# Scatters of token rows that no longer wait for one another's landing, and half of the kv copies on VectorE

## The chip, the cores and the metric

The kernel runs on one core of a Trainium2 chip. The metric is the device time of one execution in microseconds. Three runs of the kernel before took 650.41, 650.43 and 651.4 us; their median is 650.43 us. A profile of one execution shows when each engine worked: TensorE (PE, and PEld for its weight loads), VectorE (DVE), ScalarE (ACT), GpSimd (POOL) and SyncE (SP), which issues the plain loads.

## The reference

A linear attention without a softmax feeds a mixture of experts. Batch is 8, heads 8, sequence 576, head width 64; there are 8 experts of 512 to 1024 to 512.

```python
kv = np.einsum('bhsd,bhse->bhde', k, v)
out = np.einsum('bhsd,bhde->bhse', q, kv)
rms = np.sqrt(np.mean(out * out, axis=-1, keepdims=True) + 1e-06)
x = (out / rms * g_norm)                 # to (B, S, 512)
logits = np.einsum('bsd,de->bse', x, w_gate)
local_gate = 1.0 / (1.0 + np.exp(-(x @ w_local)))
# for each batch, for s in order:
fresh_e = int(np.argmax(logits[b, s]))
e = fresh_e if s == 0 or local_gate[b, s] < 0.5 else prev_e
h = np.maximum(x[b, s] @ w1[e], 0.0)
out[b, s] = softmax(logits[b, s])[e] * (h @ w2[e])
```

So each of the 4608 tokens goes through one expert, and which one is known only when its logits are.

## The kernel before

The first stage works on two batches and two heads at a time: 16 steps (`NST`), four steps (`NP`) to a group of two batches, four groups (`NGRP`). For each step s, `kv(s)` multiplies k and v on TensorE, and ACT copies the result from PSUM (`kvp`, line 390: 128 partitions, of which the lower 64 belong to the first batch of the pair and the upper 64 to the second). `kvb_of(s, t)` at line 404 lays it out in a matrix `kvb` that the product with q reads. It makes four copies per step, all on POOL: t says which half of the partitions is written, b which half is read. In the order of the program: lower half to lower half, upper to lower, lower to upper, upper to upper. ACT adds the logits' columns to the same matrix (line 431), and only then goes on to its other copies. `q_kv(s)` multiplies (lines 462, 467 and 473), and ACT writes the rows to `raw`, nine chunks (`C`) of 128 tokens for a group. POOL and ACT square them (line 511 is POOL's share), VectorE sums them (line 516).

When a group has its four steps, `rows_out` and `route` compute on VectorE which expert each token takes and at which place of a sorted list in DRAM (`xs_sorted`) its row goes (line 716). `scatter` (line 586) then writes one chunk of 128 rows with an indirect DMA from POOL. There are 36 scatters, nine to a group. Each writes the same DRAM tensor as the one before, so each waits until that one has landed.

The second stage takes rows back from `xs_sorted` with gathers. The first blocks of 128 rows of expert 0 are processed with fixed places: `ready(b)` gathers block b (line 733) and needs the groups 0 to b scattered; `scale0` scales the rows on VectorE (line 778) and `turn` transposes them on TensorE (line 790). The four blocks are called a, b, c and d here. Then come the experts 1 to 7 in the order of their numbers of rows, with `gather4` (line 745).

The order of the program is written out by hand, as strings of letters: one letter is one piece of work, and `work_of` looks up what it means. Each engine runs its own instructions in that order. The letters that matter: `0` and `1` are `kvb_of` for the next step, `n` is POOL's square of the step before, `o` is `scatter(3)`, `G` in step 14 is the scatters that are still due (they also wait for the last load of q). `LATE` replaces the string of the last steps; in steps 8 to 11 it appends a letter, in steps 8 to 10 a second `o`. In block a the string `PASS` puts seven scatters of group 2 at `a8`, in block b nine of group 3 at `b7`; `r` at `a6`, `b6` and `c3` is the gather for the next block.

As group 0 is placed at the end of step 7, its nine scatters stand six in step 8 and three in step 9. Group 1 is placed at the end of step 11: three scatters in step 12, six at `G`. Group 2: two in step 15, seven at `a8`. Group 3: nine at `b7`.

Of the kernel before, what the change touches and what calls it, by code (L numbers as in the profile page):

```python
# [22 lines left out]
def kernel(  # L23
# [14 lines left out]
    B, H, S, D = q.shape  # L38
# [7 lines left out]
    C = S // D  # L46
    W = C // 2
    NP = H // 2
    HW = D + NG
    PW = 2 * HW  # L50
    KB = PW - NG
    XO = NG
    NGRP = B // 2
    NCH = NGRP * C
    NST = NGRP * NP
# [9 lines left out]
    CLOSE = {g: g + 1 for g in range(NGRP - 1)}  # L65
    IDC = 1

    QUARTERS = range(NST - NP - 1, NST)


# [65 lines left out]
    KVB, LGC = "PP", "A"  # L136
# [150 lines left out]
    def load_q(s, b):  # L287
        if s < NST:
            qts[s, b] = load(q, lq, "qt", s, b)
# [45 lines left out]
    for x in range(2):  # L335
        rows = slice(x * D, (x + 1) * D)
# [9 lines left out]
    for b in range(2):  # L346
        rows = slice(b * D, (b + 1) * D)
# [24 lines left out]
    kvps, kqs, qTs, qls = {}, {}, {}, {}  # L372

    def half(b):
        return slice(b * D, (b + 1) * D)
# [17 lines left out]
    def blocks(s, t, o, dims):  # L393

        v_ = kvbs[s % 3][half(t), o + t * HW:]
        return bass.AP(v_.tensor, v_.offset, [v_.ap[0], *dims])

    def slot(x, b):
        return (2 * b + x) * PW

    def kvb_of(s, t):

        for b in range(2):
            copy[KVB[t]](blocks(s, t, slot(0, b) + XO, [(PW - XO, 2), (1, D)]), kvps[s][half(b)])  # L404
        done.add((s, t))

    copy = {"A": nc.scalar.copy, "D": nc.vector.tensor_copy, "P": nc.gpsimd.tensor_copy}
# [36 lines left out]
    def q_kv(s):  # L444
# [9 lines left out]
        def part(w0):  # L454
            po = ps_o.tile([P, 2, 512], F32, name="po")
            for w in range(w0, w0 + 2):
                for x in range(2):
                    for r in range(2 if s in QUARTERS else 0):
                        for b in range(2):
# [3 lines left out]
                                             kvb[half(r), o:o + HW], start=True, stop=True)  # L463
                    for b in range(0 if s in QUARTERS else 2):
                        out = po[half(b), w - w0, 0:2 * PW].rearrange("p (r e) -> p r e", r=2)
# [3 lines left out]
            if w0:  # L469
                for x in range(2):  # L470
                    for b in range(2):
# [6 lines left out]
                           po[:, :, 0:2 * PW].rearrange(  # L478
                               "p r (w e) -> p w r e" if s in QUARTERS else "p w (r e) -> p w r e",
                               e=PW))  # L480
# [4 lines left out]
        return part(0), part(2)  # L485

    bg = {}
    to_place, placed, unread = [], [], []
    done = set()

    def adv(g, n=1):

        for _ in range(n):
            while next(bg[g][0], "end") == "end":
                bg[g].pop(0)
                if not bg[g]:
                    return
# [80 lines left out]
    def scatter(n=C, after=None):  # L578

        for _ in range(min(n, len(to_place))):  # L580
            g, c, raw = to_place.pop(0)
            if not c:
                nc.gpsimd.tensor_copy(
                    raw.rearrange("p c (a w) -> p c a w", w=PW)[:, :, :, IDC],
                    tid[:, g].unsqueeze(2).to_broadcast([P, C, NP]))
            i = nc.gpsimd.indirect_dma_start(  # L586
                out=xs, out_offset=bass.IndirectOffsetOnAxis(
                    ap=place[:, g * C + c:g * C + c + 1], axis=0),
                in_=raw[:, c].bitcast(I32), in_offset=None, bounds_check=E * SPAN - 1, oob_is_err=False)
            while blank:  # L590
                tc.add_manual_dep(i.ins, blank.pop().ins.name, mybir.DependencyInfo(
                    mybir.DependencyClass.Sync, mybir.DependencyReason.DATA))
            if after:
                tc.add_manual_dep(i.ins, after.ins.name, mybir.DependencyInfo(
                    mybir.DependencyClass.Sync, mybir.DependencyReason.DATA))
                after = None
            placed.append((g, c))
            unread.append(i)

    def sum_last(dst, src):  # L600
        with nc.allow_low_precision("whole numbers below 2 ** 17"):
# [129 lines left out]
    def gather(xr, idx, groups=NGRP):  # L731
        assert len(placed) >= groups * C
        i = nc.gpsimd.indirect_dma_start(
            out=xr.bitcast(I32), out_offset=None, in_=xs,
            in_offset=bass.IndirectOffsetOnAxis(ap=idx, axis=0),
            bounds_check=E * SPAN - 1, oob_is_err=False)
        while unread:
            tc.add_manual_dep(i.ins, unread.pop().ins.name, mybir.DependencyInfo(
                mybir.DependencyClass.Sync, mybir.DependencyReason.DATA))
        return xr  # L740

    def gather4(xr, r, k, u):

        assert not unread
        i = nc.gpsimd.indirect_dma_start(  # L745
            out=xr[:, u * PW:(u + 1) * PW].bitcast(I32), out_offset=None,
            in_=xs.rearrange("t (q w) -> (t q) w", w=PW),
            in_offset=bass.IndirectOffsetOnAxis(ap=gid4[:, r - 2, u * KBM + k:u * KBM + k + 1], axis=0),
            bounds_check=E * SPAN * NP - 1, oob_is_err=False)
        if behind:  # L750
            tc.add_manual_dep(i.ins, behind.pop().ins.name, mybir.DependencyInfo(
                mybir.DependencyClass.NoSync, mybir.DependencyReason.DATA))
# [52 lines left out]
    def group(g):  # L805
# [7 lines left out]

    STEP = "Q01aKkLlnopTVsqUemwvcRYb"
    EARLY = {-1: "01TLlUeKkV", 0: "Q0aRcT1LlYUeoKkV"}
    LATE = {NST - 8: STEP + "o", NST - 7: STEP + "o", NST - 6: STEP + "o",
            NST - 5: STEP + "2", NST - 4: STEP + "34",
            NST - 3: "Q01aKkLlnTVsqUmcRYX", NST - 2: "Q01GLlTUaspcRXY",
            NST - 1: "QapwcRvosXY"}
    SLOTS = {}  # L820
# [12 lines left out]
    def work_of(i, what):  # L833


        new, nxt, now = i + 2 < NST, 0 <= i + 1 < NST, i >= 0
        if what in "pmqb":
            for g in SLOTS.get((i, what), ()):
                adv(g)
        elif what == "s" and i > 0:  # L840
            for x in range(2):
                sums(i - 1, x)
            if i % NP == 0:
                group(i // NP - 1)
        elif what == "Q" and now:
            step["a"], step["c"] = q_kv(i)
            next(step["a"])
        elif what == "R" and now:
            next(step["c"])
        elif what in "ac" and now:  # L850
            next(step[what])
            done.add((i, what))
        elif what == "K" and new:
            step["k"] = kv(i + 2)
            next(step["k"])
            for b in range(2):
                load_kv(i + 2 + LB, b)
        elif what == "k" and new:
            next(step["k"])
        elif what == "L" and nxt:  # L860
            step["l"] = logits_of(i + 1)
            next(step["l"])
        elif what == "l" and nxt:
            next(step["l"])
            done.add((i + 1, "l"))
        elif what in "01" and nxt:
            kvb_of(i + 1, int(what))
        elif what == "T" and nxt:
            for b in range(2):
                turn_q(i + 1, b)  # L870
        elif what == "U" and nxt:
            turn_last(i + 1)
        elif what == "e" and nxt:
            assert i + 1 in qls and i + 1 in qTs
            for b in range(2):
                load_q(i + 1 + LQ, b)
            if i + 1 + LQ == NST - 1:
                for x in range(len(LOADED), NW1 + NW2):
                    wload(0, x)
        elif what == "V" and new:  # L880
            turn_kv(i + 2)
        elif what == "w" and i in SPLIT:
            step["v"] = wsplit(0, SPLIT[i], True)
        elif what == "v" and i in SPLIT:
            step.pop("v")()
        elif what == "n" and i > 0:
            squares(i - 1, 0)
        elif what in "XY" and now:
            squares(i, "XY".index(what), True)
        elif what == "o":  # L890
            if i in LOADED:
                wload(0, LOADED[i])
            elif i < NST - 1:
                scatter(3)
            else:
                scatter(2)
        elif what == "G":
            right.close()
            wpool("c")
            wpool("d")  # L900
            scatter(after=latest["qt"])
        elif what == "2":
            ready(0, sm)
        elif what == "3":
            scale0(0)
        elif what == "4":
            turn(*e0[0], 0, ps_q, "pq")
# [16 lines left out]
    for i in range(-2, NST):  # L924
        if i == NST - 1:
            paced.clear()
        for what in {**EARLY, **LATE}.get(i, STEP):
            work_of(i, what)
# [384 lines left out]
    for bl in la:  # L1313
# [4 lines left out]
    i = first_block(KST - 1, {  # L1318
        2: [split[0]], 4: [split[1]], 7: [split[2]], 8: [split[3]],
        **{11 + x: [bl.scale] for x, bl in enumerate(la[:2])}, 13: [turns[0], la[2].scale],  # L1320
        14: [turns[1]], 15: [turns[2]]}, (hh, hl))
# [111 lines left out]
```

## Time and profile before

| | us |
|---|---|
| median of 3 runs (650.41 to 651.4) | 650.43 |
| the profiled execution | 648.12 |
| its span | 646.4 |
| PE busy | 554.5 (86%) |
| DVE busy | 301.3 (47%) |
| POOL busy | 264.5 (41%) |
| ACT busy | 241.6 (37%) |

The span is the time from the first to the last instruction of the profile; the profiled execution's own time is 1.7 us longer. Busy time is summed over instructions. The page cuts the span into 40 slices of 16 us: in the fifth to fifteenth slice (65 to 242 us) PE's busy share is between 1 and 7 tenths, and from the sixteenth on it is 9 tenths or more. The DMA engines are busy for 9 tenths in the first five slices.

### The profile page before, as it was taken

What the parts mean: (1) busy time and instruction counts of PE and PEld (TensorE: products, weight loads), DVE (VectorE), ACT (ScalarE), POOL (GpSimd) and SP (SyncE); (2) the same over time, 40 slices, a digit from 0 to 9 for tenths busy, and PEclk for the clock granted to TensorE, in tenths of its full rate; (3) what the DMA queues carried; (4) which work ended last, traced back from release to release, by engine and by line L of the source; (5) the groups of instructions that cost most, each with busy time, mean ns of one, the idle gap of its engine ahead of it and who ended that gap; (6) DMA issues with size and microseconds to landing.
All of it is one profiled execution on the core that took longest, in us unless ns stands there. A gap on an engine that the chain in (4) does not pass through costs nothing.

```text
span 646.4 us, 12084 instructions
## 1 busy us (share of the span) xinstructions
PE 554.5 (86%) x4720; PEld 484.1 (75%) x4720; DVE 301.3 (47%) x705; ACT 241.6 (37%) x442; POOL 264.5 (41%) x336
## 2 busy tenths in 40 slices
PE   8999515675664449999999999999999999999996
PEld 5778414564443337989898988989998898998995
DVE  1147313557242017626464637465663763756520
ACT  2678312656111125333333343433443334344321
POOL 5333233343232335627252725734544563561011
PEclk9999857989785869999999999999999999999999
DMA  9999925612243227354233423523443353352000
GB/s 325 348 345 351 348 96 184 205 68 117 93 143 148 108 70 267 105 169 129 90 111 117 129 99 121 161 74 134 133 122 122 128 161 104 130 175 77 6 33 27
DMA packets 37648, 94.96 MB, mean 147 GB/s; under 512 B 5817, under 2 KB 5817, under 8 KB 37582
## 3 DMA queue, kind: packets, MB, share of 16 engines
q1 hardware_dynamic: 26848, 61.88, 28.1%
q0 software_dynamic: 10688, 32.20, 15.0%
q8 instruction: 39, 0.64, 0.4%
q14 instruction: 27, 0.22, 0.1%
q10 hardware_dynamic: 46, 0.02, 0.0%
HBM read 73.85 MB, written 20.88 MB: 147 GB/s over the span
## 4 chain that ended last, share of the span: by engine, by line
PE 67%; issue 16%; DMA 7%; POOL 5%; ACT 1%; DVE 1%; POOLq 1%; another core or an unknown queue 0%; DVEq 0%; ACTq 0%
PE ph L947 10%; PE ph L948 10%; PE ph L942 10%; PE py L948 9%; PE py L942 9%; PE py L947 9%; DMA xs_sorted<-raw,place 5%; POOL xs_sorted L586 4%; PE po L467 3%; PE po L386 2%; PE py L995 1%; DMA xr<-xs_sorted,gi 1%; DMA out_dram<-ot,si 1%; PE pq L441 1%; PE rbank L325 1%
## 5 line engine op out<-in xcount | busy, mean ns | idle before, releaser
L745 POOL DMA_INDIRECT xr<-xs_sorted,gid x120 | 132.8, 1107 | 38.4 <-issue 35.7
L981 POOL DMA_INDIRECT out_dram<-ot,si x38 | 40.2, 1058 | 182.1 <-ACT ot L980 113.1
L1016 DVE SCALAR_TENSOR_TENSOR hl<-ph,hh 128x384 fp32r<-128x384 f32 (+3 forms) x88 | 49.5, 562 | 101.7 <-ACT hh L1015 101.7
L1015 ACT ACTIVATE hh<-ph 128x384 fp32r<-128x384 f32 (+3 forms) x88 | 44.5, 505 | 115.2 <-PE ph L948 115.2
L586 POOL DMA_INDIRECT xs_sorted<-raw,place x36 | 36.0, 999 | 87.3 <-DMA xs_sorted<-raw,place 80.4
L516 DVE TENSOR_REDUCE ms<-sq 128x9 f32<-128x576 f32 x32 | 22.6, 748 | 70.1 <-POOL sq L511 69.9
L778 DVE TENSOR_TENSOR xr<-xr 128x512 f32<-128x512 f32 x40 | 27.5, 687 | 40.6 <-DMA xr<-xs_sorted,gi 40.1
L790 PE MATMUL pt<-ident,xr 128*128 128x128 f32 x40 | 8.1, 337 | 44.2 <-DVE pe L917 38.3
L980 ACT ACTIVATE ot<-py,pe 128x512 f32<-128x512 f32 (+1 forms) x37 | 25.3, 684 | 53.5 <-issue 27.0
L790 PEld LDWEIGHTS pt<-ident,xr 128*128 128x128 f32 x40 | 5.7, 171 | 46.8 <-issue 39.0
L412 PE MATMUL pt<-ident,kvp 128*128 128x128 f32 x16 | 5.0, 313 | 29.3 <-ACT kvb L431 28.1
L404 POOL COPY kvb<-kvp 64x128 f32<-64x128 f32 x64 | 18.8, 294 | 25.5 <-ACT kvp L390 12.5
L467 PE MATMUL po<-kvb,qT 128*64 128x146 f32 x352 | 28.7, 309 | 0.0
L477 ACT COPY raw<-po 128x584 f32<-128x584 f32 x32 | 20.4, 639 | 15.2 <-PE po L473 12.7
L386 PEld LDWEIGHTS po<-vt,kt 64*64 64x64 f32 x1152 | 21.9, 142 | 5.6 <-issue 3.1
L386 PE MATMUL po<-vt,kt 64*64 64x64 f32 x1152 | 24.8, 230 | 1.4 <-issue 1.0
L412 PEld LDWEIGHTS pt<-ident,kvp 128*128 128x128 f32 x16 | 2.3, 145 | 30.4 <-ACT kvb L431 28.8
L771 ACT CAST yh<-xT 128x512 fp32r<-128x512 f32 x17 | 10.5, 620 | 38.8 <-DVE xT L767 38.8
L467 PEld LDWEIGHTS po<-kvb,qT 128*64 128x64 f32 x352 | 22.5, 145 | 3.2 <-issue 2.0
L511 POOL TENSOR_TENSOR sq<-raw 128x576 f32<-128x576 f32 x13 | 15.0, 1154 | 23.8 <-ACT raw L482 12.1
L948 PE MATMUL py<-w_0h,hl 128*128 128x512 f32 (+1 forms) x54 | 21.8, 404 | 3.1 <-DVE hl L1080 3.0
L794 ACT CAST th<-pt 128x512 fp32r<-128x512 f32 x4 | 2.3, 586 | 54.0 <-PE pt L790 54.0
(404 smaller groups left out, 1765.7 us busy)
## 6 DMA issues: line engine op xcount, KB each, us to landing
wst<-in_moe_w_dram SPq DMA_DIRECT2D x64, 512.0 KB
kt<-in_k_dram SPq DMA_DIRECT2D x32, 288.0 KB
vt<-in_v_dram SPq DMA_DIRECT2D x32, 288.0 KB
qt<-in_q_dram SPq DMA_DIRECT2D x32, 288.0 KB
xr<-xs_sorted,gid POOLq DMA_INDIRECT x120, 4.2
out_dram<-ot,si POOLq DMA_INDIRECT x40, 3.9
xs_sorted<-raw,place POOLq DMA_INDIRECT x36, 2.8
xr<-xs_sorted,gi POOLq DMA_INDIRECT x10, 6.6
```

The lines of the kernel that those rows point to most:

```text
L386: nc.tensor.matmul(pk[half(b), x, 0:D], ks[b][half(x), cd], vs[b][half(x), cd], start=(c == 0), stop=(c == C - 1))
L467: nc.tensor.matmul(out[:, :, x * HW:(x + 1) * HW], qT[:, b, w, half(x)], kvb[:, o:o + PW], start=True, stop=True)
L586: i = nc.gpsimd.indirect_dma_start(out=xs, out_offset=bass.IndirectOffsetOnAxis(ap=place[:, g * C + c:g * C + c + 1], axis=0), in_=raw[:, ...
L745: i = nc.gpsimd.indirect_dma_start(out=xr[:, u * PW:(u + 1) * PW].bitcast(I32), out_offset=None, in_=xs.rearrange("t (q w) -> (t q) w", w=PW),
L778: (engine or nc.vector).tensor_mul(xv, xv, r.unsqueeze(3).to_broadcast([P, NP, 2, D]))
L942: mm = nc.tensor.matmul(ps, ah, bh, start=(first and i == 0), stop=False)
L947: nc.tensor.matmul(ps, ah, bl, start=False, stop=False)
L948: nc.tensor.matmul(ps, al, bh, start=False, stop=(last and i == n - 1))
L980: nc.scalar.activation(ot[0:m], po[0:m], AF.Copy, scale=pe[0:m])
L981: return nc.gpsimd.indirect_dma_start(out=outf, out_offset=bass.IndirectOffsetOnAxis(ap=idx[0:m], axis=0), in_=ot[0:m], in_offset=None, bo ...
L1015: nc.scalar.activation(hh, ps, AF.Relu)
L1016: nc.vector.scalar_tensor_tensor(hl, ps[:, :, 0:nl], 0.0, hh[:, :, 0:nl].bitcast(F32), op0=ALU.max, op1=ALU.subtract)
```

## The change

Four things change. In `scatter`, a scatter is declared independent of all earlier scatters and gathers ("other rows"); in `gather`, a gather is declared independent of the scatters of later groups, and keeps its dependence on those of the groups that it reads. In the steps whose `kvb_of` has s from 8 to 13 (`CROSS`, `NP` is 4), the two copies with b = 1 go to VectorE. A letter `o` is now four scatters and does nothing from step 12 on, except two in step 15. The second `o` of steps 8 to 10 is gone. So group 0's nine scatters stand 4, 4 and 1 in steps 8, 9 and 10, and group 1's nine all at `G` in step 14.

```diff
+    CROSS = range(2 * NP, 3 * NP + 2)
...
-            copy[KVB[t]](blocks(s, t, slot(0, b) + XO, [(PW - XO, 2), (1, D)]), kvps[s][half(b)])
+            copy["D" if b and s in CROSS else KVB[t]](blocks(s, t, slot(0, b) + XO, [(PW - XO, 2), (1, D)]), kvps[s][half(b)])
...
-            placed.append((g, c))
-            unread.append(i)
+            for other in moves:
+                tc.declare_no_dep(i.ins, other.ins, reason="other rows")
+            moves.append(i)
+            placed.append(i)
...
-        while unread:
-            tc.add_manual_dep(i.ins, unread.pop().ins.name, mybir.DependencyInfo(
-                mybir.DependencyClass.Sync, mybir.DependencyReason.DATA))
+        for other in placed[groups * C:]:
+            tc.declare_no_dep(i.ins, other.ins, reason="rows of later groups")
+        moves.append(i)
...
-    LATE = {NST - 8: STEP + "o", NST - 7: STEP + "o", NST - 6: STEP + "o",
-            NST - 5: STEP + "2", NST - 4: STEP + "34",
+    LATE = {NST - 5: STEP + "2", NST - 4: STEP + "34",
...
-            elif i < NST - 1:
-                scatter(3)
-            else:
+            elif i < 3 * NP:
+                scatter(4)
+            elif i == NST - 1:
                 scatter(2)
```

## Rows read from the trace of the kernel before

**Rows 1.** The page, chain that ended last: shares of the span by engine.

```profile
PE 67%; issue 16%; DMA 7%; POOL 5%; ACT 1%; DVE 1%; POOLq 1%; another core or an unknown queue 0%; DVEq 0%; ACTq 0%
```

**Rows 2.** PE's waits, 60 to 240 us: total us, times, longest us.

```profile
PE pt L790 <- DVE pe L917: 38.3, 3, 17.9
PE pt L412 <- ACT kvb L431: 28.1, 3, 19.9
PE pt L790 <- issue: 5.5, 1, 5.5
...
PE pl L420 <- ACT kvb L431: 0.7, 1, 0.7
```

**Rows 3.** Timeline of POOL, steps 8 and 9: start, us, engine, line, idle before.

```profile
66.09 1.10 POOL L586 DMA_INDIRECT xs_sorted<-raw,place  x1 [0.29 <-POOL raw L583]
71.43 0.99 POOL L586 DMA_INDIRECT xs_sorted<-raw,place  x1 [4.24 <-DMA xs_sorted<-raw,place]
77.61 0.97 POOL L586 DMA_INDIRECT xs_sorted<-raw,place  x1 [5.20 <-DMA xs_sorted<-raw,place]
...
90.42 0.32 POOL L404 COPY kvb<-kvp 64x128 f32<-64x128 f32 x1
92.39 0.99 POOL L404 COPY kvb<-kvp 64x128 f32<-64x128 f32 x3 [1.66 <-DMA xs_sorted<-raw,place]
```

**Rows 4.** The scatters' line, L586: what POOL waited for, and landing.

```profile
  DMA xs_sorted<-raw,place: 80.4, 30
...
DMA to landing us min/median/max: 2.8/2.8/8.1
```

**Rows 5.** Timeline of ACT in step 9.

```profile
72.49 0.27 ACT L390 COPY kvp<-po 128x128 f32<-128x128 f32 x1 [0.32 <-PE po L386]
92.72 0.18 ACT L431 COPY kvb<-pm 64x36 f32<-64x36 f32 x1 [19.96 <-POOL kvb L404]
```

**Rows 6.** Timeline of POOL, small copies at L583, step 14, and a gather.

```profile
65.55 0.25 POOL L583 COPY raw<-tid 128x36 f32<-128x36 f32 x1
...
139.97 1.03 POOL L586 DMA_INDIRECT xs_sorted<-raw,place  x1 [0.28 <-POOL kvb L404]
...
158.16 1.18 POOL L583 COPY raw<-tid 128x36 f32<-128x36 f32 x1
...
242.75 1.01 POOL L733 DMA_INDIRECT xr<-xs_sorted,gi  x1 [0.31 <-issue]
```

**Rows 7.** Timeline of PE: two steps, a restart, block a's start, three transposes.

```profile
57.26 1.22 PE L467 MATMUL po<-kvb,qT 128*64 128x146 f32 x16
...
63.38 1.22 PE L467 MATMUL po<-kvb,qT 128*64 128x146 f32 x16
...
94.83 2.21 PE L467 MATMUL po<-kvb,qT 128*64 128x146 f32 x16
...
146.03 0.51 PE L942 MATMUL ph<-w_0h,th 128*128 128x512 f32 x1
...
171.88 1.12 PE L790 MATMUL pt<-ident,xr 128*128 128x128 f32 x4 [6.26 <-DVE pe L917]
...
202.48 1.09 PE L790 MATMUL pt<-ident,xr 128*128 128x128 f32 x4 [14.22 <-DVE pe L917]
...
235.12 1.09 PE L790 MATMUL pt<-ident,xr 128*128 128x128 f32 x4 [17.86 <-DVE pe L917]
```

**Rows 8.** The chain in order of time: a gather, issue to landing.

```profile
230.81 3.48 DMA xr<-xs_sorted,gi
```

**Rows 9.** Timeline of DVE: a copy, a two-input instruction, group 3's places.

```profile
100.11 0.15 DVE L568 COPY raw<-r 128x72 f32<-128x72 f32 x1
...
158.01 1.23 DVE L227 TENSOR_TENSOR w_1l<-wst,w_1h 128x1024 fp32r<-128x1024 f32 x1
...
180.58 0.23 DVE L716 TENSOR_REDUCE place<-rk 128x9 int32<-128x72 f32 x1
```

**Rows 10.** A 20 us window: busy us of PE, PEld, DVE, ACT, POOL; granted clock; DMA.

```profile
80.00:100.00 20.00, 6.21 (x113) 4.76 (x115) 3.85 (x10) 5.22 (x12) 6.41 (x10) 0.55 0.36 124
```

More of the change, by code (lines that the diff above doesn't have):

```diff
@@ L487 @@
     bg = {}
-    to_place, placed, unread = [], [], []
+    to_place, placed, moves = [], [], []
     done = set()
@@ L736, in gather @@
             bounds_check=E * SPAN - 1, oob_is_err=False)
-        while unread:
-            tc.add_manual_dep(i.ins, unread.pop().ins.name, mybir.DependencyInfo(
-                mybir.DependencyClass.Sync, mybir.DependencyReason.DATA))
+        for other in placed[groups * C:]:
+            tc.declare_no_dep(i.ins, other.ins, reason="rows of later groups")
+        moves.append(i)
         return xr
     def gather4(xr, r, k, u):
-        assert not unread
         i = nc.gpsimd.indirect_dma_start(
```

## The prediction

> **What bounds the kernel now.** I read the chain of waits first, then TensorE's waits in the stretch that the chain points at, then POOL's timeline there. Over the whole span the chain is two thirds PE [rows 1], so most of the kernel is already bound by TensorE; the rest is "issue", DMA and POOL, and all of that lies between 66 and 235 us. TensorE's waits there show two kinds of stall [rows 2]. In the attention steps it stands 28.1 + 0.7 us behind ACT's L431; in the expert-0 blocks it stands 38.3 us, in three waits, behind VectorE's scaling of gathered rows. Both lead to one place. POOL's timeline shows each scatter followed by an idle time that ends with the landing of the scatter before it [rows 3]: 30 waits, 80.4 us, with a landing of 2.8 us on idle DMA engines [rows 4]. While q, k and v are still loading, scatters start 5.3 and 6.2 us apart [rows 3]. POOL runs its program in order, so the next step's kv copies stand behind the scatters. There the reader sees a detail that the forecast hangs on: of four kv copies the first runs at once, and the second waits until the last scatter has landed (1.66 us idle), the third and fourth with it [rows 3]. ACT's L431 waits 19.96 us for these copies [rows 5], and TensorE's transposes wait for PSUM that ACT empties. In the blocks the gather that feeds the next block stands behind seven or nine serial scatters.
>
> **The change, part by part.**
>
> *Scatters no longer wait.* Two waits go. Behind L431: 28.8 us. In the blocks: 38.3 us, if every gather is now in time. That I check from block a's first matmul as zero, with a cadence of 1.3 us per indirect DMA (1.01 busy, 0.31 between, from gathers that already follow each other without a wait) [rows 6]. Step 14's first scatter stood 6.1 us ahead of zero (139.97 against 146.03) [rows 6, 7]. Nine of them (it was six) last to +5.6, two of group 2 to +8.3; the gather for block b needs the ninth landed (+8.4), issues until +9.5 and lands 3.5 us after its start [rows 8], +11.9. Block a's work before that transpose ended 6.26 us ahead of 171.88, at +19.6 [rows 7], so there are 7 us to spare. Seven scatters then end at +18.6. From transpose to transpose TensorE works 202.48 - 14.22 - 171.88 = 16.4 us in b and 235.12 - 17.86 - 202.48 = 14.8 in c [rows 7], less 1.5 each for the clock (below), so its next two appointments are +34.5 and +47.8. Block c's gather stands behind block a's output scatter and may issue until +30, ten us after the transpose that block a's last products follow. Group 3's places are known 8.9 us after the first transpose (180.81 against 171.88) [rows 7, 9], less the clock's 1.2: +27.3. Nine scatters: +39. Landed +41.8; last gather landed +45.3, scaled and checked in +46.3. That is in time by 1.5 us on idle DMA engines and late by about as much if the two landings take a loaded 4.5; I charge 0.7. Register reads and expert 1's first weights follow the same places and have the rest of block c.
>
> *The clock comes back.* After each of these stalls TensorE restarts at the lower of its two levels (1.2 and 2.4 GHz): the granted clock of 80 to 100 us is 0.55 of full speed [rows 10], and 16 matmuls that last 1.22 us last 2.21 [rows 7]. That is 1.0 us there, and some 0.5 in the smaller instructions around it. Five stalls (two long ones in the steps, three in the blocks) at 1.5 make 7.5 us. Bounds: 0, if other stalls still keep the clock low, and 10.
>
> So 28.8 + 38.3 + 7.5 = 74.6 us can go. Next is what comes back.
>
> *Half of the kv copies on VectorE.* They are the two whose source is the second batch's half. VectorE's cost of one is not in the trace: 0.15 us is its copy of 128x72 [rows 9], 0.32 the same copy on POOL [rows 3]. I take 0.2, two a step; this hides under TensorE's 6.1 us a step (57.26 to 63.38) [rows 7], except where VectorE is still at the step before's work; I charge 1.0 us in all. POOL keeps two copies: lower half to lower half, which the trace shows running at once, and lower half to upper half. Whether this last one waits for a landing by itself the trace does not show: today it runs behind the second copy, which has waited already. Bounds: no wait, 0; a full wait in each step after scatters. I take the wait, since the nearest row, the second copy, is also one that goes from one half to the other.
>
> Its price: in step 8 four scatters start at 66.09 and end near 70.9. A single landing under load took 4.0 and 4.9 us after the issue's end (67.19 to 71.2, 72.42 to 77.3) [rows 3]; with 4.5 the last lands at 75.4, and ACT goes on at 75.8 instead of 72.8, when its copy of kvp is done [rows 5]: 3.0 us. Then one square (1.1 us) and four more scatters, 77.2 to 82.0, landed 86.5, against ACT's wish at 72.8 + 6.1 + 3.0 = 81.9: 4.9 with the copy. The ninth alone costs 0.7. Before step 12's copies stands a gather, as it did before, which I cost at nothing; up to 4 us if its landing now delays the squares from which that step's VectorE chain starts (TensorE's 5.5 us wait on "issue" [rows 2] is that chain, and stays). Sum 8.6, bounds 0 and 13.
>
> A rule of the Trainium skill speaks against the move. The trace shows POOL's small copy at L583 taking 0.25 us alone and 1.18 us while VectorE ran a 1.23 us instruction with two SBUF inputs [rows 6, 9]. The Trainium skill ("GPSIMD Engine Reference", section Key points) says that POOL shares its SBUF interfaces with VectorE and contends with such instructions and with its two-port modes. By that rule each new VectorE copy could also hold POOL for its own length, which would make the sum some 1.2 us larger; by the row alone nothing is added, as a copy has one input.
>
> *Four a step, none in step 12.* Group 0 goes 4, 4, 1 instead of 6, 3; group 1's first three move from step 12 into step 14, counted above. POOL in step 8 then has 5.2 us of scatters, 0.7 of copies and 1.1 of squares, 7.0 against a 6.1 us step; step 10 has slack for the excess.
>
> **Sum.** 74.6 - 8.6 - 1.0 - 0.7 = 64.3 us. The profiled execution took 648.12 us (span 646.4); it becomes 583.8. The median of the runs is 2.3 us higher, 650.43, so the forecast is 586. From the last of the three transposes on (235 us) nothing changes: 411 us with TensorE busy throughout.
>
> **Rivals.**
>
> *No copy on POOL waits any more.* Then 8.6 comes off: 577.5. For it: only the second copy is seen to start a wait. Against: today's order hides whether the third would.
>
> *Queued scatters are slow.* If four scatters in flight beside the loads land one after another at the loaded pace of 5.3 and 6.2 us [rows 3], the last of step 8 lands near 89 and ACT loses 16 us there, then 4 in step 10: 20 instead of 8.6, 597. For it: loaded landings reach 8.1 us [rows 4]. Against: those were measured one at a time, so nothing says that they add up. The Trainium skill ("DMA: Bandwidth & Descriptors", section Queues, rings and completion order) has the DMA engines take turns between queues packet by packet, which would let the four land together; no run here shows four in flight.
>
> *The landings stay in series (slower).* If something other than the declared order holds each scatter until the one before has landed, none of the 74.6 us goes, and step 14 has nine instead of six ahead of the gather for block b, which ends a TensorE wait today: three times 2.8 + 0.3 us [rows 4] is 9.3, less some 2 for copies that no longer stand behind step 12's three: 658. It decides as soon as scatters are more than 2.5 us apart. For it: nothing in the rows but that every scatter today waits. Against: gathers from the same queue follow each other after 0.31 us [rows 6].
>
> **How the numbers follow.** Forecast (kv copy waits, 580 to 592): 0.47. No wait (572 to 580): 0.34. Slow queue (592 to 606): 0.12. Series, 658: 0.03; 0.02 for series with no net effect; 0.02 for below 571. The range 571 to 604 leaves out the last three and the end of the slow queue, under 2 in 10. About 0.2% is what can be told from no change here. Faster 0.95, same 0.02, slower 0.03.
>
> **What would show it.** In POOL's timeline L586 should stand 1.3 us apart in all five places, and its idle time behind DMA xs_sorted fall from 80 us to a few. L404 on POOL should appear twice a step, the second one idle until the last landing, some 4.5 us after the last issue in steps 9 and 10: if that gap is absent, the first rival holds. TensorE's wait before L790 on the scaled rows should be gone twice and at most 2 us the third time; the granted clock should stay at its upper level from 80 us on but for step 12. Block a should start near 123 us and the third transpose stand near 171 us instead of 235. The prediction is wrong if scatters stay 3 us apart, if SP's loads of k and v become what TensorE waits for, or if the stretch after that transpose is not 411 us.

## The result and the profile after

The changed kernel takes 581.33 us (median of 4 runs, 579.72 to 585.42) against 650.8 for the kernel before on the same chip: ratio 0.894, 95% interval 0.889 to 0.899. The profiled execution took 580.01 us, its span is 578.3, 68.1 us less than before. 586 was forecast, with a range of 571 to 604.

The page first: busy time of each engine, and the chain that ended last by engine (before: [rows 1]).

```profile
PE 546.9 (95%) x4720; PEld 478.0 (83%) x4720; DVE 305.7 (53%) x717; ACT 241.9 (42%) x442; POOL 264.7 (46%) x324
...
PE 64%; issue 4%; DMA 2%; DVE 1%; POOLq 1%; ACT 0%; POOL 0%; another core or an unknown queue 0%; DVEq 0%; ACTq 0%
```

"issue", DMA and POOL had 28% of the chain and have 6%. The same 4720 matmuls are busy for 546.9 us instead of 554.5: those 7.6 us are the clock, net: its mean granted level rises from 0.935 to 0.981 of full speed. POOL's timeline in steps 8 and 9 (before: [rows 3]; L586 is now L587, L404 is L405; columns: start, us, engine, line, idle before):

```profile
65.78 1.10 POOL L587 DMA_INDIRECT xs_sorted<-raw,place  x1 [0.29 <-POOL raw L584]
67.18 0.98 POOL L587 DMA_INDIRECT xs_sorted<-raw,place  x1 [0.30 <-issue]
...
69.74 0.97 POOL L587 DMA_INDIRECT xs_sorted<-raw,place  x1 [0.30 <-issue]
70.71 0.66 POOL L405 COPY kvb<-kvp 64x128 f32<-64x128 f32 x2
71.45 1.15 POOL L512 TENSOR_TENSOR sq<-raw 128x576 f32<-128x576 f32 x1
72.75 1.03 POOL L587 DMA_INDIRECT xs_sorted<-raw,place  x1 [0.15 <-issue]
```

Scatters start 1.28 us apart, and the two copies left on POOL follow the fourth at once: no scatter and no copy waits for a landing any more. (Gathers still do, as they must.) The scatters' own line shows the same (before: 80.4 us behind landings, [rows 4]); a landing now takes 5.0 us in the median, as four to nine are in flight:

```profile
  issue: 8.5, 29
...
DMA to landing us min/median/max: 2.8/5.0/7.6
```

TensorE's waits from 60 to 190 us (total, times, longest; before: [rows 2]):

```profile
PE pt L792 <- issue: 6.6, 2, 6.5
PE pt L792 <- DVE pe L918: 3.8, 1, 3.8
...
PE po L463 <- issue: 2.1, 2, 1.5
PE po L387 <- issue: 1.5, 1, 1.5
```

L432's 28.1 us are gone (0.8 us left under it), and of the 38.3 us behind scaled rows one wait of 3.8 remains. TensorE's marks on the way (before: [rows 7], where the first stood at 130.31, the second at 146.03 and the last at 235.12):

```profile
103.43 1.08 PE L792 MATMUL pt<-ident,xr 128*128 128x128 f32 x4 [6.49 <-issue]
...
117.55 0.50 PE L943 MATMUL ph<-w_0h,th 128*128 128x512 f32 x1
...
166.76 0.63 PE L792 MATMUL pt<-ident,xr 128*128 128x128 f32 x4 [3.81 <-DVE pe L918]
```

So 28.5 us came in the attention steps and 39.9 between block a's start and the third transpose. From there to the end it is 411.5 us, as before (411.3). The window that stood at a clock of 0.55 [rows 10] is now

```profile
80.00:100.00 20.00, 13.19 (x356) 11.21 (x355) 11.90 (x31) 10.95 (x30) 7.86 (x13) 0.90 0.96 361
```

It is 0.90 and not full because the 62 matmuls at L387 that start at 90.12, behind a stop of 1.5 us (the "issue" rows above), run at a granted 0.50: they take 2.05 us, and 1.22 us at 1.00 in another run (f1 below).

### The profile page after: what moved, and what is told of

It is laid out like the page before. It is cut to its first block, busy times and chain, and to the rows that moved or that the text cites. A ratio compares the mean times of both kernels' runs of the same rounds, so it can differ in the third digit from the quotient of the medians.

```text
span 578.3 us, 12098 instructions
## 1 busy us (share of the span) xinstructions
PE 546.9 (95%) x4720; PEld 478.0 (83%) x4720; DVE 305.7 (53%) x717; ACT 241.9 (42%) x442; POOL 264.7 (46%) x324
## 4 chain that ended last, share of the span: by engine, by line
PE 64%; issue 4%; DMA 2%; DVE 1%; POOLq 1%; ACT 0%; POOL 0%; another core or an unknown queue 0%; DVEq 0%; ACTq 0%
PE ph L948 11%; PE ph L943 11%; PE ph L949 11%; PE py L949 10%; PE py L948 10%; PE py L943 10%; PE py L996 1%; DMA out_dram<-ot,si 1%; DMA xr<-xs_sorted,gi 1%; PE pt L792 1%; DVE xr L780 0%; DVE xl L797 0%; POOLq L1381 0%; ACT xh L796 0%; POOLq L1430 0%
## 5 line engine op out<-in xcount | busy, mean ns | idle before, releaser
L587 POOL DMA_INDIRECT xs_sorted<-raw,place x36 | 37.7, 1046 | 11.3 <-issue 8.5
L405 POOL COPY kvb<-kvp 64x128 f32<-64x128 f32 x52 | 15.5, 299 | 28.9 <-ACT kvp L391 23.8
L468 PE MATMUL po<-kvb,qT 128*64 128x146 f32 x352 | 26.6, 293 | 0.0
L387 PEld LDWEIGHTS po<-vt,kt 64*64 64x64 f32 x1152 | 21.7, 145 | 5.9 <-issue 3.6
L387 PE MATMUL po<-vt,kt 64*64 64x64 f32 x1152 | 24.2, 232 | 1.5 <-issue 1.5
L468 PEld LDWEIGHTS po<-kvb,qT 128*64 128x64 f32 x352 | 20.9, 136 | 2.8 <-issue 1.6
L769 DVE STREAM_TRANSPOSE xT<-xr 128x512 f32<-128x512 f32 x30 | 21.2, 707 | 0.4
L943 PE MATMUL py<-w_1h,hh 128*128 128x512 f32 (+1 forms) x54 | 21.4, 396 | 0.0
L943 PE MATMUL py<-w_0h,hh 128*128 128x512 f32 (+1 forms) x54 | 21.3, 395 | 0.0
L948 PE MATMUL py<-w_0l,hh 128*128 128x512 f32 (+1 forms) x54 | 21.3, 395 | 0.0
L949 PE MATMUL py<-w_1h,hl 128*128 128x512 f32 (+1 forms) x54 | 21.1, 390 | 0.0
```

Of the source, the lines that this page charges most:

```text
L387: nc.tensor.matmul(pk[half(b), x, 0:D], ks[b][half(x), cd], vs[b][half(x), cd], start=(c == 0), stop=(c == C - 1))
L468: nc.tensor.matmul(out[:, :, x * HW:(x + 1) * HW], qT[:, b, w, half(x)], kvb[:, o:o + PW], start=True, stop=True)
L587: i = nc.gpsimd.indirect_dma_start(out=xs, out_offset=bass.IndirectOffsetOnAxis(ap=place[:, g * C + c:g * C + c + 1], axis=0), in_=raw[:, ...
L943: mm = nc.tensor.matmul(ps, ah, bh, start=(first and i == 0), stop=False)
L948: nc.tensor.matmul(ps, ah, bl, start=False, stop=False)
L949: nc.tensor.matmul(ps, al, bh, start=False, stop=(last and i == n - 1))
```

## The experiments

Three sets were run, each beside the kernel before. In the first the kernel before took 650.1 us, as beside the changed kernel, and ratios can be set against 0.894. The second and third ran on two other chips, where the kernel before took 660.7 and 661.3 us and TensorE stops for a reason of its own (f1 below); their ratios are compared with each other only.

**All copies on POOL.**

```diff
-    CROSS = range(2 * NP, 3 * NP + 2)
+    CROSS = ()
```

> The changed kernel with all four kv copies of a step on POOL again (VectorE copies none). Theory: the copy that starts a wait is the one whose source is the second batch's half. It stands behind the scatters of its step and idles until the last of them has landed, some 4.5 us after its issue, in steps 8 to 10 (3.0, 4.9 and 0.7 us by the forecast's working, and about as much again where a gather or nine scatters stand ahead, steps 12 and 13): 587 to 596 us, with ACT's L432 idle 8 to 15 us behind these copies. Rival (the copies matter as work only): four copies of 0.3 us take the place of two, 581 to 583 us, and no idle time on POOL ahead of L405 that ends with a landing.

593.45 us, ratio 0.911 (0.907 to 0.915): 12 us slower than the changed kernel. POOL in step 8:

```profile
71.16 1.18 POOL L587 DMA_INDIRECT xs_sorted<-raw,place  x1 [0.30 <-issue]
72.35 0.30 POOL L405 COPY kvb<-kvp 64x128 f32<-64x128 f32 x1
79.28 0.99 POOL L405 COPY kvb<-kvp 64x128 f32<-64x128 f32 x3 [6.64 <-DMA xs_sorted<-raw,place]
```

The second copy idles 6.64, 5.64 and 3.77 us in three steps, and TensorE stands 12.8 us behind L432. The theory holds; the rival, the copies as work alone, said 581 to 583 us.

**The other pair on VectorE.**

```diff
-            copy["D" if b and s in CROSS else KVB[t]](...)
+            copy["D" if t and s in CROSS else KVB[t]](...)
```

> The changed kernel with the other pair of copies on VectorE: those that write the upper half (t = 1), so that POOL keeps the two that write the lower half, one from each half of the source. As many copies on either engine as in the changed kernel. Theory (it is the source's upper half that waits): POOL's second copy idles until the scatters have landed, 586 to 595 us, as with all four on POOL. Rival 1 (any two copies off POOL do it; what counts is POOL's load): 580 to 583 us. Rival 2 (the copy from one half to the other waits): the same as the theory here, but then the changed kernel, which keeps such a copy on POOL, should have shown the wait too.

590.33 us, ratio 0.908 (0.905 to 0.912). POOL keeps one copy from each half of the source, both into the lower half, and the second waits:

```profile
70.77 0.30 POOL L405 COPY kvb<-kvp 64x128 f32<-64x128 f32 x1
78.05 0.29 POOL L405 COPY kvb<-kvp 64x128 f32<-64x128 f32 x1 [6.98 <-DMA xs_sorted<-raw,place]
```

So it is not POOL's load: as many copies were moved as in the change, and of its 12 us only 3 were gained.

**One copy on VectorE** (second set).

```diff
-            copy["D" if b and s in CROSS else KVB[t]](...)
+            copy["D" if b and not t and s in CROSS else KVB[t]](...)
```

> The changed kernel with only one copy of a step on VectorE: the one from the upper half of the source to the lower half of the blocks (t = 0, b = 1). POOL keeps three, among them the one from upper half to upper half, which in the two runs before always came behind the copy that had waited. Theory 1 (the source's upper half is what waits): that copy idles until the scatters have landed, ACT's L432 idles some 12 us again, 588 to 594 us. Theory 2 (only the move from the upper to the lower half waits): no idle time that ends with a landing, 580 to 584 us, and the second copy on VectorE was not needed.

Ratio 0.928 (0.922 to 0.934) on a slower chip, so the trace decides:

```profile
72.78 0.65 POOL L405 COPY kvb<-kvp 64x128 f32<-64x128 f32 x2
79.03 0.30 POOL L405 COPY kvb<-kvp 64x128 f32<-64x128 f32 x1 [5.61 <-DMA xs_sorted<-raw,place]
```

The two from the lower half run at once, also the one that crosses to the upper half; the one from upper to upper waits. With the two runs before, the half that is read decides and not the crossing. Both copies of the second batch had to leave POOL.

The trace also shows where the wait comes from. In step 8 of the run with all copies on POOL, POOL's own stream of instructions has two semaphore waits (POOLq) at the copies' line, between the first copy and the second:

```profile
L405 POOLq EVENT_SEMAPHORE  x2: 43/43/43, 78.1 to 79.2; - x2
```

They name four semaphores (110 to 113), the ones that the step's four scatters raise when they land. In steps 8 to 10 of the changed kernel no copy has such a wait, on POOL or on VectorE. So the wait is written in the program. Why the program has it ahead of a copy that reads the upper half, and not of the others, is open.

**Scatters in series again.** Only the scatters' declaration is taken out; the one in `gather` stays.

```diff
-            for other in moves:
-                tc.declare_no_dep(i.ins, other.ins, reason="other rows")
```

> The changed kernel in everything, but each scatter waits again for the landing of the one before it: four a step, nine in step 14, VectorE's copies. Theory (the waiting is the whole of the gain; the placement gives nothing by itself): 650 to 662 us, the forecast's own price for landings in series. Rival (a good part of the gain is the copies on VectorE and the emptied step 12): 620 to 645 us.

647.13 us, ratio 0.9945 (0.991 to 0.998), just under the theory's range. Scatters wait 80.6 us for landings again, and TensorE's waits (60 to 240 us) are nearly those of before:

```profile
PE pt L790 <- DVE pe L916: 47.0, 3, 17.8
PE pt L413 <- ACT kvb L432: 21.1, 2, 13.0
```

All but some 3 us of the gain hang on this declaration. The forecast's rival for this case put 658: its loss in the blocks (9.3 us for three more scatters ahead of a gather) was nearly right, as block a's start to the third transpose grew by 8.1 (139.68 to 236.88), but the steps gave back 6.4 us and not 2.

**The declarations alone.** The kernel before with no scatter waiting, `CROSS` empty, `scatter(3)` twice in steps 8 to 10 and once in step 12:

```diff
-            elif i < 3 * NP:
-                scatter(4)
-            elif i == NST - 1:
+            elif i < NST - 1:
+                scatter(3)
+            else:
                 scatter(2)
```

> The kernel before with only the declarations that scatters do not depend on each other: three scatters a step as before (six and three a group, three in step 12), all kv copies on POOL. Theory: most of the gain is here; what is missing against the changed kernel is the copy that waits for landings (5 to 15 us, now in step 12 too): 588 to 602 us. Rival (the three parts of the change need each other, as the copies' wait eats what the scatters give): 610 us or more.

590.91 us, ratio 0.908 (0.904 to 0.912): 59 of the 69 us. The placement makes no difference that shows while all copies are on POOL (0.911 with four a step).

**The old placement with VectorE's copies** (second set; the edit of the run before, with `CROSS` kept).

> The changed kernel with the scatters where they were before: six and three a group in steps 8 to 10, three in step 12, 15 behind. Scatters still do not wait and VectorE has its copies. Theory (the placement is worth nothing by itself once nothing waits: POOL has room either way, and step 12 is held by VectorE's chain): within 2 us of the changed kernel, 579 to 584 us. Rival (four a step spread the load on the DMA engines and an emptied step 12 lets its squares start earlier): 585 to 590 us, with TensorE's wait of step 12 above 8 us or ACT's L432 behind POOL again.

Ratio 0.916 (0.912 to 0.921), the fastest of its set. The changed kernel was not in that set; the run below, which differs from it only behind step 15, had 0.928. So nothing shows that the new placement is worth anything. That the old one was faster fits f1 below, where scatters in step 14 cost TensorE time on such a chip, but the stand-in has an edit of its own, so this is not shown. A trace detail shows why step 12 was emptied: `CROSS` ends before the copies for step 14, and these wait behind step 12's three scatters:

```profile
105.59 0.31 POOL L405 COPY kvb<-kvp 64x128 f32<-64x128 f32 x1
112.58 0.99 POOL L405 COPY kvb<-kvp 64x128 f32<-64x128 f32 x3 [6.68 <-DMA xs_sorted<-raw,place]
```

**Expert 1's weights later** (second set).

```diff
+        if after:
+            tc.add_manual_dep(fetched[-1].ins, after.ins.name, mybir.DependencyInfo(
+                mybir.DependencyClass.Sync, mybir.DependencyReason.DATA))
...
-            wload(*to_load.pop(0))
+            wload(*to_load.pop(0), after=None if i else placed[-1])
```

> The changed kernel with one wait added on SP: the first weights of expert 1 are loaded only when the last scatter has landed (they were issued at 151.2 us, four of 512 KB, while the last nine scatters were under way; the first split of them starts at 170.2). Theory (the last gather is late because these loads hold the DMA engines: 7.3 us from the last scatter's issue to the gather, against 2.8 of a landing on idle engines): the gather comes 3 to 4.5 us earlier, TensorE's third wait on the scaled rows falls from 3.8 us to under 0.7, 576 to 578.5 us. Rival 1 (nine scatters in flight are slow by themselves): the gather still comes 6 us or more behind the last scatter, the wait stays above 2.5 us, 580 to 583 us. Rival 2 (the wait goes, but expert 1 starts late by as much): 580 to 583 us, with TensorE waiting for L231 at its start.

Ratio 0.928 (0.923 to 0.933); a wait of 2.3 us on scaled rows is left. The gather did start sooner, 3.9 us behind the last scatter's end (181.80 to 185.69) instead of 7.3, but VectorE then got its rows after 8.1 us (193.82) instead of 3.5. So the forecast of under 0.7 us of wait failed; f3 below has the same edit.

**Scaling early in step 12** (second set).

```diff
-            NST - 5: STEP + "2", NST - 4: STEP + "34",
+            NST - 5: STEP + "2", NST - 4: STEP.replace("s", "3s") + "4",
```

> The changed kernel with VectorE's scaling of the first gathered rows in step 12 (three instructions, 0.98 us) ahead of the step's squares and softmax instead of behind them. The rows landed by about 91 us, VectorE idles until 91.4 us, and the softmax chain ends at 102.7; TensorE's transposes stand behind the scaling until 103.4 (6.5 us without a match). Theory (that wait is VectorE's program order, the term that the forecast left as it was): it falls below 1 us and most of it is kept, since the next thing that TensorE needs of VectorE is a product that would now come at about 103.4, when its operand is 0.7 us old: 575 to 578 us. Rival (the step is held by the chain anyway, and the same time is waited in the next step or at block a's start): 580 to 583 us.

Ratio 0.920 (0.915 to 0.926). The wait is gone from TensorE's list, but there was no run of the changed kernel to compare with. The third set was made for that: f1 is the changed kernel again, f2 has the early scaling, f3 has it and expert 1's weights later.

> The changed kernel itself once more, so that the three others of this set are compared with it on the same chip. In the set before, all four kernels and the kernel before were slower than in the first set (before 660.7 against 650.1 us), and TensorE stopped there in the middle of groups of matmuls while POOL issued scatters. Theory (that was that chip; the kernel has no such stops of its own): 579 to 586 us, ratio 0.890 to 0.900. Rival (the changed kernel is that variable everywhere): above 590 us.

> The changed kernel with VectorE's scaling of the first gathered rows ahead of step 12's squares and softmax, again, now beside the changed kernel. Theory: TensorE's wait of 6.5 us in step 12 is VectorE's program order; it falls below 1 us and 3 to 6 us of it stay gained. Rival (the next product waits instead): within 1.5 us of the changed kernel.

> The changed kernel with both: scaling early in step 12, and expert 1's first weights loaded only behind the last scatter's landing. Theory (both waits, 6.5 and 3.8 us, are what is named, and they add): 7 to 10 us under the changed kernel, no wait of TensorE above 1 us on the scaled rows of the last block, and the last gather 3 to 4.5 us behind the last scatter's issue instead of 7.3. Rival 1 (the loads have nothing to do with the late gather): as the one before, gather 6 us or more behind. Rival 2 (late weights are late for expert 1): slower than the one before by 1 us or more.

*f1*: 616.41 us, ratio 0.932 (0.927 to 0.937). The rival holds: on this chip the same kernel gains 45 us and not 69. Its nine scatters of step 14, 1.3 us apart as ever, show why. The same stretch, in the windows of the first changed run and then of f1 (us; busy of PE, PEld, DVE, ACT, POOL; clock; DMA share; GB/s):

```profile
110.20:121.60 11.40, 9.86 (x226) 8.01 (x224) 7.18 (x25) 9.60 (x23) 8.96 (x9) 1.00 0.55 213
```

```profile
119.40:130.70 11.30, 5.83 (x79) 3.94 (x78) 3.08 (x14) 2.93 (x8) 8.82 (x9) 0.77 0.55 212
```

POOL and the DMA engines do the same work, but TensorE runs 79 matmuls instead of 226. In f1 its timeline drips, a few matmuls every 0.74 us in the middle of one group, with operands long there:

```profile
121.52 0.35 PE L463 MATMUL po<-kvb,qT 64*64 64x73 f32 x4 [0.44 <-issue]
122.29 0.35 PE L463 MATMUL po<-kvb,qT 64*64 64x73 f32 x3 [0.42 <-issue]
123.05 0.33 PE L463 MATMUL po<-kvb,qT 64*64 64x73 f32 x2 [0.41 <-issue]
```

It drips from 121.5 to 132.5 us and again from 138.5, each time some 2 us behind the scatters' issue (119.4 to 130.7, and from 136.4), and runs freely between. Block a starts at 145.37 instead of 117.55: 18.6 us were lost in steps 13 and 14, and 9.2 before step 12's transpose.

*f2*: 610.57 us, ratio 0.921 (0.916 to 0.927). Step 12's transpose comes at 104.84 instead of 112.65, with no idle time before it, block a starts 5.5 us earlier and the third transpose 7.4. That wait was VectorE's program order, and most of what it cost is kept.

*f3*: 608.83 us, ratio 0.912 (0.904 to 0.920), below f1's interval and the best of the set; of f2 it can't be told apart (its six runs lie between 598.4 and 617.76 us). The loads did move behind the scatters, but on top of the gather. POOL's last gather, and VectorE's first use of its rows:

```profile
180.83 1.06 POOL L739 DMA_INDIRECT xr<-xs_sorted,gi  x1 [0.31 <-PE pt L1081]
```

```profile
188.74 0.69 DVE L783 TENSOR_TENSOR xr<-xr 128x512 f32<-128x512 f32 x1 [3.69 <-DMA xr<-xs_sorted,gi]
```

That is 7.9 us, against 3.5 (162.42 to 165.97) in the first changed run, where the loads were through by then, and 5.2 in f1. From the last scatter's issue to the scaling it is 12.8 us here, 11.9 in the first changed run and 11.0 in f1. On this chip the edit had little to win: TensorE's wait on these rows was 0.4 us in f1 and 1.4 in f2, and here it is 3.1. The theory's cause is half right: either of the two transfers is slow when the loads stand beside it, and held back until the last scatter has landed they stand beside the gather. Making them wait for the gather's landing was not tried.

**Fewer matmuls in steps 11 and 12** (f4, third set).

```diff
-    QUARTERS = range(NST - NP - 1, NST)
+    QUARTERS = range(NST - 3, NST)
```

> The changed kernel with steps 11 and 12 using matmuls over all 128 rows with 146 columns (as steps 0 to 10 do) instead of twice as many of 64 rows and 73 columns. In the changed kernel TensorE stops three times there, 0.62, 1.50 and 1.48 us, in the middle of such groups, where no operand changes. Theory (it waits for its own instructions, which come slower while loads keep the DMA engines full): the two stops among these matmuls go or fall under 0.5 us together, the third, among other matmuls, may stay; 0 to 2 us faster. Rival (it waits for q, k and v, as the forecast named it): the stops stay, up to 1 us slower or faster.

Ratio 0.923 (0.917 to 0.929), median 619.48 us of runs from 610.14 to 625.61, so nothing can be said of its time. TensorE's "issue" stops from 75 to 105 us, f1 and then this run:

```profile
PE po L387 <- issue: 2.5, 2, 2.0
PE po L463 <- issue: 0.7, 1, 0.7
PE pl L421 <- issue: 0.6, 1, 0.6
```

```profile
PE po L387 <- issue: 0.4, 1, 0.4
```

3.8 us become 0.4 with as many loads of q, k and v. This alone does not decide: TensorE stood 4.0 us behind ACT's L432 in this stretch, which it did not in f1, and the loads took 61% of the DMA engines' time instead of 73%. Where the stops fall does decide, as the next section shows.

## Why the prediction was right, and where it was wrong

*Scatters no longer wait*: right in mechanism and size. 28.0 of 28.8 us behind L432 and 34.5 of 38.3 us in the blocks went, and with the declarations undone (in series) both came back.

*The clock*: 7.5 us forecast, 7.6 measured as TensorE's busy time.

*What bounds the kernel*: that all of the chain's "issue", DMA and POOL lies between 66 and 235 us was read too broadly. Some five sixths do; "issue" is also 4.7% of the 411 us behind, and is so after the change, and it is most of the 6% that is left.

*Half of the kv copies on VectorE*: wrong. The forecast let the copy from the lower to the upper half, left on POOL, wait for landings, 8.6 us in all, because the only row of a waiting copy also crossed halves. It does not wait; the rival "no wait on POOL" is what happened. The row allowed two readings, the half that is read or the crossing, and the forecast took the second. The two copies that were moved are the ones that wait, which the runs with all, one and the other pair of copies show. The wait stands in the program, as the semaphore waits above show; why it is there is open. VectorE's twelve copies took 0.25 us in the median (0.2 assumed) and up to 1.04. POOL was not held by them: of its copies in these steps only one took over 0.32 us, 0.56 at 77.66, beside a VectorE instruction with two inputs.

*Why 581 and not that rival's 577.5, then*: the forecast left TensorE's 5.5 us of step 12 as they were (6.5 now; f2 shows they could go), charged 0.7 for the last gather (3.8), and had nothing for three stops of 0.62, 1.50 and 1.48 us in steps 11 and 12. Together that is 7.7 us more than charged (1.0, 3.1 and 3.6), where 8.6 had been charged for the copy: two errors that nearly cancel, so that 586 came out close is in part luck. Some 3 us by which the profiled execution came out better still (580.0 against 583.8, less the 0.9 of these two) were not traced. Block a started at 117.55 instead of 123; from there to the third transpose it took 49.2 us, 48 forecast.

The last gather is the term that was mis-sized. Its two landings were put at 2.8 to 4.5 us each. From the last scatter's end at 155.09 to the gather it took 7.3, of which 6.4 until the landing (161.5); the second landing took the 3.5 that the prediction's sum has:

```profile
154.12 0.97 POOL L587 DMA_INDIRECT xs_sorted<-raw,place  x1 [0.30 <-issue]
155.39 0.97 POOL L982 DMA_INDIRECT out_dram<-ot,si  x1 [0.30 <-issue]
162.42 1.05 POOL L736 DMA_INDIRECT xr<-xs_sorted,gi  x1 [6.05 <-DVE hl L1081]
```

The row names VectorE, whose instruction ended at 161.53; the profile has a wait of POOL's queue at L736 on the last scatter's semaphore until 161.5. TensorE was also ready sooner than forecast, 45.4 us after block a's start instead of 47.8. Expert 1's weights moved at the same time; the forecast had given them "the rest of block c" without asking what they meet. The queues from 152 to 156 us (packets, MB, share):

```profile
q1 hardware_dynamic: 235, 0.90, 80.0%
q0 software_dynamic: 64, 0.22, 18.8%
```

Sixteen engines were busy, and the loads had four fifths of them. The Trainium skill ("DMA: Bandwidth & Descriptors", section Queues, rings and completion order) has an engine take turns between queues packet by packet; packets of nearly one size (0.90 MB in 235, 0.22 in 64) would by that come in equal numbers while both queues have work. Over these 4 us they do not, and in the next 4 they nearly do (232 and 200); whether the scatters' queue had packets ready on every engine all the time is not shown, so this neither bears the rule out nor refutes it.

*Step 9's copies*: the forecast's mark of some 4.5 us idle before the second copy is absent, as its first rival said it would be. *The prediction's point that loads of k and v could become what TensorE waits for*: the stops came, but in the middle of a group of matmuls:

```profile
88.35 0.60 PE L463 MATMUL po<-kvb,qT 64*64 64x73 f32 x22 [1.50 <-issue]
...
93.64 0.39 PE L387 MATMUL po<-vt,kt 64*64 64x64 f32 x10 [1.48 <-issue]
```

They are its instructions. The three stops end at 82.64, 88.35 and 93.64 us, and from each to the next TensorE has exactly 256 instructions: 126 matmuls, 126 weight loads and 4 semaphore instructions. f1 and f2, on another chip, stop ahead of the very same matmuls, the 1729th and the 1855th of the 4720 (f1: 0.73 and 2.03 us, at 96.62 and 101.64). The Trainium skill ("Runtime: NRT & Kernel Launch", section Instruction fetch mechanics) says that an engine's instructions come in blocks of 16 KiB, 256 instructions, through a DMA queue of their own, and that crossing from one to the next is mostly hidden. The trace has such packets:

```profile
q8 instruction: 39, 0.64, 0.5%
```

One of them ends 1.3 to 1.6 us ahead of each restart (at 81.19, 87.01 and 92.04). Beside full DMA engines they are not hidden here.

## What to carry to other kernels

When a queue's transfers touch different rows, the order between them is the first thing to take away: the declarations alone were worth 59 us here. When one of several like instructions waits, list which operand half each of them reads and writes before saying which ones will wait after a change: one row fits more than one rule. The profile also lists the semaphore waits of an engine's queue by line; they tell which instruction carries the wait. And where transfers no longer wait, they overlap with loads that used to stand clear of them; ask for each appointment that is met by a few us what else is on the DMA engines then.

## What was not expected of the hardware

On two of three chips TensorE starved while scatters were issued back to back. On the chip of the third set it ran 79 matmuls in 11.3 us beside nine scatters, 226 in 11.4 us on the first chip, with the same DMA load (0.55); the second set's chip shows the same drip. The kernel before, whose scatters stand apart, is only 1.6 and 1.7% slower on those chips. Late blocks of instructions, the cause of the three stops, do not explain the drip: in f1 it starts inside a block of 256 and not at its end, and the one instruction packet that lands in it (at 124.94) does not end it, as matmuls go on dripping to 132.5. Its cause, and what differs between the chips, is open.
